# Attention with memory and a long convolution in one kernel: wider transfers, weights on a second queue, one operation for four products, row halves, and a new order

## The chip, the cores and the metric

The kernel runs on one core of a Trainium2 chip. The metric is the time of one execution in microseconds of the device (us). The engines are TensorE (PE in the profile; PEld is its loading of weights), VectorE (DVE), ScalarE (ACT), GpSimd (POOL) and SyncE (SP), whose queue (SPq) issues transfers. Each engine works through its own list in order and waits there for what the others deliver.

## The reference

Two independent parts whose outputs stand side by side, 2048 rows of 576 columns each, in bf16.

```python
def _A_ref(x, wq, wk, wv, wo, beta):       # S = 2048, D = 576, H = 32, Dh = 18, N = 4 segments of L = 512
    q, k, v = (x @ wq), (x @ wk), (x @ wv)           # split in heads and segments
    phi = lambda t: jnp.where(t > 0, t + 1.0, jnp.exp(t))
    g = _sigmoid(beta)
    for s in range(N):
        p = _softmax(qs @ ks.T * scale + mask)       # causal inside a segment
        a_dot = p @ vs
        a_mem = (phi(qs) @ M) / (phi(qs) @ z + 1e-06)
        o = g * a_mem + (1.0 - g) * a_dot
        M = M + phi(ks).T @ vs;  z = z + phi(ks).sum()
    return concat(o) @ wo
def _B_ref(q, k, v, shift_k, ssm_k, ssm_D):
    k_shift = short_conv(k, shift_k)                 # 4 taps
    kv = k_shift * v
    y = irfft(rfft(kv) * rfft(ssm_k)) + kv * ssm_D   # along the 2048 rows, per channel
    return q * y
```

## The kernel before

Part A goes through four segments of 512 rows. Per segment, x comes in transposed (tiles xT, line 737, one transposing load for each of five channel blocks); TensorE forms q and k for five blocks of up to 126 channels (seven heads of 18) and v for four row blocks. The contraction over 576 channels is five products of 128: the last block starts at channel 448, and the weights' overlapping rows are zeroed (line 607). q and k are copied from PSUM into tiles dn, written to a DRAM scratch (qk_scratch, line 768) and read back as pad tiles (line 778), in which each head has 32 partitions, so that four heads share TensorE's rows. Per group of four heads (hg, eight in a segment) there are three score steps (products at line 966, ScalarE's exponential at line 973 into P tiles, GpSimd's causal mask at line 980), the product with V, whose column of ones gives the sums of the softmax, a copy into a tile ou and a write to a_scratch (line 1026). The sums are read from a_scratch (cs, line 1040), inverted (lines 1046 and 1047) and spread by a product (R). The outputs come back in am tiles (line 1068), are scaled (line 1074), the memory part is added (line 1083), and the projection with wo follows. The memory part needs phi of q and k (lines 798, 804, 810), one operation for each of both.

Part B convolves k with its four taps as products with diagonal matrices (dg, line 404), multiplies by v (line 422), and writes kv to a DRAM scratch. The long convolution is a factored Fourier transform by products, in five channel groups. In each octave the transforms H (of the kernel) and X (of kv) are copied from PSUM and multiplied: lines 525, 529 and 530 give the four products of real and imaginary halves in tiles PQ. The inverse follows (Z), one transposing transfer per group (CT, line 558), a last product, and the multiplication by q (line 585).

The order of all steps is a table in the file: TURN says which step comes when, ENGINE which engine does it, SLOT which buffer it gets. Tiles rotate in a fixed number of slots (SLOTS), for example three pad tiles and five xT tiles. All transfers are issued on SP's queue in the order of the table. Nothing is planned at run time; an engine waits if what it needs is late.

## Time and profile before

| | |
|---|---|
| median of 3 runs | 341.86 us (341.12 to 344.55) |
| span of the profiled execution | 344.8 us |
| TensorE busy | 270.6 us (78%), granted clock 0.931 in the mean |
| VectorE busy | 244.9 us (71%) |
| ScalarE busy | 247.3 us (72%) |
| GpSimd busy | 105.8 us (31%) |
| transfers on the queues of SP | 71.7% of 16 engines' span, 51.99 MB |

A share of the span is an average over a start that fills the tables, a long middle in which both parts run mixed, and an end in which only the last segment and group are left. The chain that ended last follows, from the last instruction back, what each step was waiting for; its shares tell what the span was spent on. A time in a row is the start, counted from the span's begin, if it stands first.

### The profile page before, as it was taken

To read this page: it belongs to the slowest core of one execution; us is meant where nothing else is said; L and a number is where in the kernel's file an instruction comes from. 1 tells how busy PE (TensorE), PEld (TensorE's weight loads), DVE (VectorE), ACT (ScalarE), POOL (GpSimd) and SP (SyncE) were. 2 spreads that over 40 slices of the span, in tenths; PEclk is the share of its full clock that TensorE was granted. 3 is DMA by queue.
4 is the path that set the end of the run, shared out by engine and by line. 5 is a ranking of instruction groups with operands and counts; after the bars stand their busy time and mean duration, and the time that the engine had idled before them with its cause. 6 is when DMAs were issued, how large, how long until landed. Compare 5 with 4: busy or idle time off the path is not lost.

```text
span 344.8 us, 9276 instructions
## 1 busy us (share of the span) xinstructions
PE 270.6 (78%) x3850; PEld 167.3 (49%) x3855; DVE 244.9 (71%) x400; ACT 247.3 (72%) x290; POOL 105.8 (31%) x150
## 2 busy tenths in 40 slices
PE   1759789788978468989988978989877878868256
PEld 0335366345636325645645664545456646627123
DVE  4675677679999518877988884868768868866250
ACT  0484998587889425958979896998896849969302
POOL 9370022333332211222214235443601414413200
PEclk9998999899999969999999998999999969967858
DMA  5987889759969968892599855963694656573623
GB/s 138 279 115 155 191 130 155 196 110 163 193 182 195 188 153 212 155 205 60 164 192 130 248 92 163 197 171 92 135 165 132 130 165 120 95 177 80 139 57 84
DMA packets 132184, 52.58 MB, mean 152 GB/s; under 512 B 112430, under 2 KB 124910, under 8 KB 132142
## 3 DMA queue, kind: packets, MB, share of 16 engines
q1 hardware_dynamic: 132142, 51.99, 71.7%
q8 instruction: 30, 0.49, 0.7%
q14 instruction: 12, 0.10, 0.1%
HBM read 22.39 MB, written 17.01 MB: 114 GB/s over the span
## 4 chain that ended last, share of the span: by engine, by line
PE 30%; DMA 20%; ACT 18%; DVE 15%; SPq 12%; issue 5%; POOL 0%; DVEq 0%; ACTq 0%
PE PS L136 18%; ACT P L973 14%; PE PS L138 8%; DMA am<-a_scratch 5%; SPq L737 5%; DMA pad<-qk_scratch 5%; PE PS L966 3%; DMA CT<-Z 3%; DMA a_scratch<-ou 2%; DMA X<-in_B_v_dram 2%; DMA skb<-in_B_shift_k_dram 2%; DVE am L1074 2%; DVE dn L144 1%; ACT A L142 1%; DVE xs L315 1%
## 5 line engine op out<-in xcount | busy, mean ns | idle before, releaser
L973 ACT ACTIVATE P<-PS 128x1024 bf16<-128x1024 f32 x160 | 154.2, 1035 | 43.6 <-PE PS L966 33.4
L980 POOL TENSOR_SCALAR_AFFINE_SELECT P<-P 128x512 bf16<-128x512 bf16 (+1 forms) x112 | 79.5, 725 | 199.1 <-ACT P L973 116.8
L966 PE MATMUL PS<-pad 18*128 18x128 bf16 (+3 forms) x512 | 35.9, 314 | 12.5 <-DMA pad<-qk_scratch 5.7
L136 PE MATMUL PS<-xT,wq 128*126 128x512 bf16 (+1 forms) x100 | 28.4, 415 | 11.6 <-DMA xT<-in_A_x_dram 11.1
L966 PEld LDWEIGHTS <-pad 18*128 18x128 bf16 x512 | 11.2, 93 | 36.2 <-issue 26.8
L136 PE MATMUL PS<-wo,am 126*128 126x288 bf16 (+1 forms) x160 | 26.7, 322 | 2.4 <-DVE am L1083 1.1
L136 PE MATMUL PS<-X,dg 128*128 128x512 bf16 x75 | 21.6, 416 | 7.6 <-DMA X<-in_B_k_dram 6.3
L138 PE MATMUL PS<-P,V 128*32 128x256 bf16 (+3 forms) x512 | 23.8, 307 | 4.4 <-ACT P L973 1.6
L136 PE MATMUL PS<-xT,wk 128*126 128x512 bf16 (+1 forms) x100 | 26.6, 400 | 0.5 <-DMA wk<-in_A_wk_dram 0.4
L144 DVE CAST dn<-PS 126x1024 bf16<-126x1024 f32 (+1 forms) x16 | 19.5, 1219 | 9.4 <-ACT P L973 4.4
L138 PE MATMUL PS<-G,PQ 64*128 64x128 bf16 (+1 forms) x640 | 23.5, 225 | 3.3 <-ACT P L973 1.7
L138 PEld LDWEIGHTS <-Ft 128*64 128x64 bf16 x704 | 21.2, 114 | 7.2 <-issue 6.4
L138 PEld LDWEIGHTS <-PQ 64*128 64x128 bf16 (+1 forms) x640 | 20.5, 102 | 8.4 <-issue 7.0
L136 PE MATMUL PS<-wv,xT 128*128 128x288 bf16 x160 | 22.6, 291 | 2.2 <-ACT V L142 1.5
L138 PE MATMUL PS<-A,Ft 128*64 128x128 bf16 (+1 forms) x640 | 22.6, 223 | 2.0 <-ACT P L973 1.0
L138 PE MATMUL PS<-W,xs 128*64 128x128 bf16 x576 | 20.9, 220 | 4.1 <-ACT P L973 2.3
L136 PEld LDWEIGHTS <-wq 128*126 128x126 bf16 (+1 forms) x100 | 13.3, 141 | 21.2 <-issue 9.4
L144 DVE CAST A<-PS 128x1024 bf16<-128x1024 f32 x18 | 21.6, 1217 | 2.7 <-PE PS L138 2.6
L422 DVE TENSOR_TENSOR X<-PS,X 128x1024 bf16<-128x1024 f32 x10 | 12.1, 1222 | 15.7 <-PE PS L136 14.2
L138 PEld LDWEIGHTS <-xs 128*64 128x64 bf16 x576 | 17.9, 109 | 9.0 <-issue 7.8
L136 PEld LDWEIGHTS <-am 126*128 126x128 bf16 (+1 forms) x160 | 16.8, 109 | 11.2 <-issue 3.0
L804 ACT ACTIVATE fe<-dn 126x512 bf16<-126x512 bf16 (+1 forms) x30 | 19.1, 639 | 2.4 <-DVE fk L810 1.9
(127 smaller groups left out, 427.5 us busy)
## 6 DMA issues: line engine op xcount, KB each, us to landing
pad<-qk_scratch SPq DMA_DIRECT2D x32, 256.0 KB
a_scratch<-ou SPq DMA_DIRECT2D x32, 128.0 KB
qk_scratch<-dn SPq DMA_DIRECT2D x16, 252.0 KB
out_dram<-oA SPq DMA_DIRECT2D x16, 144.0 KB
xs<-in_B_ssm_k_dram SPq DMA_DIRECT2D x4, 512.0 KB
kv_scratch<-X SPq DMA_DIRECT2D x4, 512.0 KB
xs<-kv_scratch SPq DMA_DIRECT2D x4, 512.0 KB
q<-in_B_q_dram SPq DMA_DIRECT2D x8, 256.0 KB
```

Source lines behind the costliest of these rows:

```text
L136: self.nc.tensor.matmul(out, lhsT=lhsT, rhs=rhs, start=start, stop=stop)
L138: self.nc.tensor.matmul(out, lhsT=lhsT, rhs=rhs, start=start, stop=stop, tile_position=pos)
L142: self.nc.scalar.copy(out=out, in_=in_)
L144: self.nc.vector.tensor_copy(out=out, in_=in_)
L315: v.tensor_scalar(out=self.i32(ix), in0=self.i32(it), scalar1=self.t(self.bcol)[:, 0:1], scalar2=self.t(off)[:, 0:1], op0=ALU.mult, op1=AL ...
L422: self.nc.vector.tensor_tensor(out=self.t(kv)[:, sl], in0=self.psf(pc), in1=self.t(vT)[:, sl], op=ALU.mult)
L737: self.nc.sync.dma_start_transpose(out=self.t(b)[:], in_=self.A_x[0, L * s:L * s + L, c0:c0 + P])
L804: self.nc.scalar.activation(out=self.t(fe)[0:M], in_=self.t(dense[m])[0:M, w_, :], func=ACT.Exp)
L966: nc.tensor.matmul(o, lhsT=t[r, 1, q0:q0 + P], rhs=t[r, 0, q0:L], start=True, stop=True, tile_position=(32 * j, 0))
L973: self.nc.scalar.activation(out=out2(jj), in_=self.psf(pso[jj]), func=ACT.Exp, scale=scale)
L980: self.nc.gpsimd.affine_select(out=ap, in_=ap, compare_op=ALU.is_ge, fill=0.0, base=0, pattern=pat + [[1, P]], channel_multiplier=-1)
L1074: self.nc.vector.tensor_tensor(out=self.t(b)[0:M], in0=self.psf(pR)[0:M], in1=self.t(b)[0:M], op=ALU.mult)
```

## The change

- x of a segment comes in by two transposing loads, one of 512 channels and one of channels 448 to 575; a small copy inside SBUF puts the last 64 channels on the lower 64 partitions too. xT is one tile of one slot.
- The weights wq, wk, wv, wo, the short kernel, D and beta are loaded by ScalarE's queue (16 issues, 13 of them ahead of the first exponential); all else stays on SP's. The last 64 rows of wq are on the upper 64 partitions, those of wk on the lower, wv has half of its columns on each. The zeroing of line 607 is gone.
- q and k of a block: eight products of 128 rows and then one pair of products of 64 rows, q on the upper, k on the lower half of TensorE's rows, into different PSUM banks. v likewise, with its two column halves.
- A head's 18 channels lie as 9 and 9 in its 32 partitions (rows 0 to 8 and 16 to 24); a transfer's outer dimension is then 14 and not 7. Score products run over 25 rows, 7 of them zero. There are two scratches for q and k in turn, each filled with zeros once (four fills, not two). Pads come in pairs of head groups (16 loads of 512 KB for 32 of 256 KB), in two slots.
- ou holds a pair of head groups: 16 writes to a_scratch for 32. The softmax sums go from ou to cs by transfers inside SBUF, 16 for 9. Reciprocals are one operation a segment in the first three segments, two in the last (five for nine).
- The denominators of the memory part are written twice (six writes for three), since a head is in two halves.
- phi of q and k is one operation of 1024 where both are wanted (segments 1 and 2).
- The four spectral products are one operation of 2048 that reads each half of X and H twice.
- dg and the addition of the memory part may run on GpSimd; the fills of V with ones move from the program's first place into the order.
- SLOTS change (PQ two of 2048 and X two for PQ four of 1024; Hx 3 for 4, fe, rs, rb, rc one for two, am 5 for 6), and TURN, ENGINE and SLOT are new throughout.

Core of the diff:

```diff
-                    self.nc.sync.dma_start_transpose(out=self.t(b)[:], in_=self.A_x[0, L * s:L * s + L, c0:c0 + P])
+                self.nc.sync.dma_start_transpose(out=self.t(xT)[:, 0:4, :], in_=self.A_x[0, L * s:L * s + L, 0:512])
+                self.nc.sync.dma_start_transpose(out=self.t(xT)[:, 4, :], in_=self.A_x[0, L * s:L * s + L, 448:576])
+                self.nc.sync.dma_start(out=self.t(xT)[0:64, 4, :], in_=self.t(xT)[64:128, 4, :])
...
-                        for t in range(5):
-                            self.mm(o[0:M, w_, :], self.t(wt)[:, t, 126 * m:126 * m + M], self.t(xT[t])[:], t == 0, t == 4)
+                        for t in range(4):
+                            self.mm(o[0:M, w_, :], self.t(wt)[:, t, 126 * m:126 * m + M], x[:, t, :], t == 0, False)
+                        if w_ == 1:
+                            for i in range(2):
+                                w = self.t(self.w[("wq", "wk")[i]])
+                                r = slice(64 - 64 * i, 128 - 64 * i)
+                                self.mm(o[0:M, i, :], w[r, 4, 126 * m:126 * m + M], x[r, 4, :], False, True, (64 - 64 * i, 0))
...
-                    src = bass.AP(d.tensor, d.offset + hg * 128 * 1024, [[1024, P], [1, 1024]])
+                    src = bass.AP(d.tensor, d.offset + hp * 256 * 1024, [[1024, P], [128 * 1024, 2], [1, 1024]])
...
-                    self.nc.vector.tensor_tensor(out=self.t(Pt)[:], in0=self.t(X)[:], in1=self.t(H)[:], op=ALU.mult)
-                    self.nc.vector.tensor_tensor(out=x[:, 0:512], in0=x[:, 0:512], in1=h[:, 512:1024], op=ALU.mult)
-                    self.nc.vector.tensor_tensor(out=x[:, 512:1024], in0=x[:, 512:1024], in1=h[:, 0:512], op=ALU.mult)
+                        d = [[512, 2], [0, 2]]
+                        return bass.AP(a.tensor, a.offset, [list(a.ap[0]), d[i], d[1 - i], [1, 512]])
+                    self.nc.vector.tensor_tensor(out=self.t(Pt)[:].rearrange("p (a b f) -> p a b f", a=2, b=2), in0=dup(self.t(X), 0),
+                                                 in1=dup(self.t(H), 1), op=ALU.mult)
...
-                    src = bass.AP(d.tensor, d.offset + (4 * ha * 32 + DH) * L, [[32 * L, 4 * (hb - ha)], [P, 4], [1, P]])
-                    self.nc.sync.dma_start(out=self.t(cs)[16 * ha:16 * hb, :], in_=src)
+                        a = self.rows(self.t(ou), 25, 0, [(1, 32, 4), (0, P, 8), (0, 1, P)])
+                        self.nc.sync.dma_start(out=self.t(cs)[16 * (hg - 1):16 * (hg - 1) + 32, :], in_=a)
...
-    nV=6, splits=[[(0, 4), (4, 8)], [(0, 4), (4, 8)], [(0, 4), (4, 8)], [(0, 4), (4, 6), (6, 8)]]
+    nV=6, splits=[[(0, 8)], [(0, 8)], [(0, 8)], [(0, 4), (4, 8)]]
```

The lists of the engines, at three places. First SP's queue at the start of the program. Before, five loads of xT, two of wq and one of wk stand ahead of these rows (wk, wv: weights; X: transposed k and v of part B; P: the zeros; dn: q and k; skb, Dt: small constants):

```order
L615 DMA wk<-in_A_wk_dram 64x576
L612 DMA wv<-in_A_wv_dram 128x4x576
L615 DMA wv<-in_A_wv_dram 64x576
L721 DMA qk_scratch<-P_4_141 32x4x1792 x2
L375 DMA skb<-in_B_shift_k_dram 128x4
L370 DMA skb<-in_B_shift_k_dram 128x4x4
L389 DMA_TRANSPOSE X_1_100<-in_B_k_dram 128x2048
L768 DMA qk_scratch<-dn_119 7x18x1024
L364 DMA Dt<-in_B_ssm_D_dram 4x144x1
L768 DMA qk_scratch<-dn_120 7x18x1024
L392 DMA_TRANSPOSE X_0_99<-in_B_v_dram 128x2048
L778 DMA pad_130<-qk_scratch 128x1024
```

Now these are its first rows:

```order
L763 DMA_TRANSPOSE xT_113<-in_A_x_dram 128x4x512
L766 DMA_TRANSPOSE xT_113<-in_A_x_dram 128x512
L769 DMA xT_113<-xT_113 64x512
L398 DMA_TRANSPOSE X_0_99<-in_B_k_dram 128x2048
L750 DMA qk_scratch_160<-P_0_129 32x4x1792
L401 DMA_TRANSPOSE X_1_100<-in_B_v_dram 128x2048
L807 DMA qk_scratch_160<-dn_115 14x9x1024
L807 DMA qk_scratch_160<-dn_114 14x9x1024
L464 DMA xs_103<-in_B_ssm_k_dram 128x32x64
L817 DMA pad_121<-qk_scratch_160 128x2x1024
```

The weights and small constants are gone from it, the transposed load of v stands ahead of the first write of q and k, and the first pad is the tenth transfer instead of the twenty-first.

Second, SP's queue near the end. Before, the last two writes of ou were followed by the transpose of Z and then by the sums cs and the last two am:

```order
L1068 DMA am_142<-a_scratch 126x1x512
L1026 DMA a_scratch<-ou_157 128x512
L1026 DMA a_scratch<-ou_158 128x512
L558 DMA_TRANSPOSE CT_98<-Z_101 128x32x64
L1040 DMA cs_167<-a_scratch 32x1x128
L1068 DMA am_143<-a_scratch 72x1x512
L1068 DMA am_145<-a_scratch 126x1x512
```

Now (am_136 to am_138 are the last three of five):

```order
L1076 DMA a_scratch<-ou_148 128x2x512
L601 DMA out_dram<-q_102 64x16x128
L1076 DMA a_scratch<-ou_147 128x2x512
L1083 DMA cs_155<-ou_147 32x1x128
L601 DMA out_dram<-q_102 64x16x128
L1118 DMA am_136<-a_scratch 126x1x512
L1154 DMA out_dram<-oA_150 128x576
L1118 DMA am_137<-a_scratch 72x1x512
L1118 DMA am_138<-a_scratch 126x1x512
L576 DMA q_102<-in_B_q_dram 64x16x64
L567 DMA_TRANSPOSE CT_98<-Z_101 128x32x64
```

The sums follow the last write at once, and the transpose of Z stands behind the am loads.

Third, VectorE in the first octaves of the spectral products (PS is PSUM, Hx the kernel's transform, PQ the products). Before:

```order
L144 CAST PQ_112<-PS 128x1024
L798 TENSOR_SCALAR fq_125<-dn_119 126x512
L525 TENSOR_TENSOR PQ_111<-PQ_112,Hx_106 128x1024
L144 CAST PQ_109<-PS 128x1024
L529 TENSOR_TENSOR PQ_112<-PQ_112,Hx_106 128x512
L530 TENSOR_TENSOR PQ_112<-PQ_112,Hx_106 128x512
```

Now:

```order
L539 TENSOR_TENSOR PQ_110<-X_109,Hx_106 128x2048
L411 MEMSET X_1_100 128x8
L413 TENSOR_SCALAR dg_112<-ident,skf 128x128 x4
L145 CAST dn_114<-PS 126x1024
L145 CAST Hx_107<-PS 128x1024
L539 TENSOR_TENSOR PQ_111<-X_109,Hx_106 128x2048
```

Three operations have become one, and X has tiles of its own.

## Rows read from the trace of the kernel before

**Rows 1.** Busy times by stretch; columns: stretch, length, engines, clock, DMA share, GB/s.
```profile
0.00:36.00 36.00, 22.08 (x107) 12.43 (x108) 21.96 (x53) 16.14 (x20) 16.91 (x27) 0.95 0.80 174
36.00:320.00 284.00, 236.97 (x3666) 147.92 (x3672) 216.09 (x338) 226.85 (x264) 87.94 (x122) 0.95 0.75 155
```

**Rows 2.** The page's part 4: shares of the chain that ended last.
```profile
PE 30%; DMA 20%; ACT 18%; DVE 15%; SPq 12%; issue 5%; POOL 0%; DVEq 0%; ACTq 0%
PE PS L136 18%; ACT P L973 14%; PE PS L138 8%; DMA am<-a_scratch 5%; SPq L737 5%; DMA pad<-qk_scratch 5%; PE PS L966 3%; DMA CT<-Z 3%; DMA a_scratch<-ou 2%; DMA X<-in_B_v_dram 2%; DMA skb<-in_B_shift_k_dram 2%; DVE am L1074 2%; DVE dn L144 1%; ACT A L142 1%; DVE xs L315 1%
```

**Rows 3.** Timeline of the start; columns: start us, us, engine, line, operation.
```profile
23.13 4.09 SPq L392 DMA_TRANSPOSE X<-in_B_v_dram  x1
...
27.35 0.49 SPq L778 DMA_DIRECT2D pad<-qk_scratch  x1
...
36.23 1.94 ACT L973 ACTIVATE P<-PS 128x1024 bf16<-128x1024 f32 x2 [0.48 <-PE PS L966]
```

**Rows 4.** Instructions on one tile (PQ); columns: minimum/median/maximum ns.
```profile
L525 DVE TENSOR_TENSOR PQ<-PQ,Hx x18: 675/685/1146, 69.8 to 311.1; 128x1024 bf16<-128x1024 bf16 x18
L529 DVE TENSOR_TENSOR PQ<-PQ,Hx x18: 404/417/1258, 73.0 to 311.8; 128x512 bf16<-128x512 bf16 x18
```

**Rows 5.** Groups by line; columns: count, busy us, mean ns, idle before.
```profile
L144 DVE CAST A<-PS 128x1024 bf16<-128x1024 f32 x18 | 21.6, 1217 | 2.7 <-PE PS L138 2.6
...
L804 ACT ACTIVATE fe<-dn 126x512 bf16<-126x512 bf16 (+1 forms) x30 | 19.1, 639 | 2.4 <-DVE fk L810 1.9 <-DVE dn L144 0.4
...
L1046 DVE RECIPROCAL rc<-cs 64x128 f32<-64x128 bf16 (+1 forms) x9 | 8.5, 943 | 8.2 <-DMA cs<-a_scratch 8.2
...
L1083 DVE TENSOR_TENSOR am<-am,nm 126x512 bf16<-126x512 bf16 (+1 forms) x10 | 5.4, 547 | 0.1
```

**Rows 6.** Timeline of TensorE's products around 55 us.
```profile
54.87 1.29 PE L136 MATMUL PS<-xT,wq 128*126 128x512 bf16 x5
56.09 0.39 PE L966 MATMUL PS<-pad 18*128 18x512 bf16 x4
56.42 1.29 PE L136 MATMUL PS<-xT,wk 128*126 128x512 bf16 x5
```

**Rows 7.** The chain that ended last, in order of time; columns: start, us, what.
```profile
106.85 5.76 DMA pad<-qk_scratch
...
122.30 1.13 SPq L737
...
204.96 2.74 DMA xT<-in_A_x_dram
...
251.11 3.78 PE PS L136 x30
...
255.86 3.38 DMA a_scratch<-ou
...
259.31 1.96 DMA cs<-a_scratch
...
271.93 6.25 DMA pad<-qk_scratch
```

**Rows 8.** Two lines of transposing loads on SyncE's queue; minimum/median/maximum ns.
```profile
L737 SPq DMA_TRANSPOSE xT<-in_A_x_dram x20: 1127/1252/2441, 0.8 to 205.0; - x20
...
L392 SPq DMA_TRANSPOSE X<-in_B_v_dram x5: 1956/2678/4087, 23.1 to 148.3; - x5
```

**Rows 9.** Timeline of SyncE's queue near the end.
```profile
321.92 1.69 SPq L1026 DMA_DIRECT2D a_scratch<-ou  x2
323.65 3.08 SPq L558 DMA_TRANSPOSE CT<-Z  x1
326.85 1.24 SPq L1040 DMA_DIRECT2D cs<-a_scratch  x1
328.47 1.46 SPq L1068 DMA_DIRECT2D am<-a_scratch  x2
```

**Rows 10.** What SyncE's queue waited for; columns: us in total, times, longest.
```profile
SPq L778 <- PE PS L966: 6.6, 7, 1.5
```

More of the change, by code (lines that the diff above doesn't have):

```diff
@@ L160, in dma, with q, rows @@
         work = nb / pk * per[k] / eng
-        return self.g.add(name, {"SP": issue}, fn, r=r, w=w, prio=prio, lat=lat, work=work * self.p["dmaw"], al=al)
+        return self.g.add(name, {q: issue for q in queues}, fn, r=r, w=w, prio=prio, lat=lat, work=work * self.p["dmaw"], al=al)
+    def q(self, e):
+        return self.nc.sync if e == "SP" else self.nc.scalar
+    def rows(self, t, row, off, dims):
+        a = t[:]
+        n = a.ap[0][0]
+        return bass.AP(a.tensor, a.offset + row * n + off, [[k * n, c] if isr else [k, c] for isr, k, c in dims])
     def pe(self, name, cols, nmm, fn, r, w, prio, mode="F", al=()):
@@ L627, in build_a_consts, with vz @@
-                self.dma(nm + "4", l2, [], [(b, 1)], pr, 72 * 1152, pk=1152)
-        self.Vones = []
-        for i in range(p["nV"]):
-            pass
+                    self.q(e).dma_start(out=self.t(b)[0:72, 4, :], in_=self.A_wo[504:576, :])
+                self.dma(nm, l1, [], [(b, 0)], pr, 504 * 1152, pk=1152, queues=CQ)
+                self.dma(nm + "4", l2, [], [(b, 1)], pr, 72 * 1152, pk=1152, queues=CQ)
+        self.vz = F("vz")
+        def vz(e):
+            for i in range(SLOTS["V"]):
+                self.nc.gpsimd.memset(self.tiles[("V", i)][:], 1.0)
@@ L633, in build_a_consts, with lb0 @@
+        g.add("vz", {"POOL": 2.5}, vz, w=[self.vz], prio=p["prio_w"] - 30)
         self.gg = F("gg")
         bt = F("bt")
-        def lb(e):
-            src = bass.AP(self.A_beta.tensor, self.A_beta.offset, [[1, 32], [0, 4], [1, 1]])
-            self.nc.sync.dma_start(out=self.t(bt)[:], in_=src)
-        self.dma("beta", lb, [], [bt], p["prio_w"] + 20, 256, pk=64)
+        gd = Buf(None, "gd")
+        def lb0(e):
+            b, d = self.A_beta, self.tiles["gd"][:]
+            for u in range(2):
+                self.q(e).dma_start(out=bass.AP(d.tensor, d.offset + u, [[8, 4], [2, 4], [1, 1]]),
+                                    in_=bass.AP(b.tensor, b.offset + 4 * u, [[8, 4], [1, 4], [1, 1]]))
@@ L713, in build_a @@
             pieces[hg] = pcs
-        qd = Buf(None, "qd")
+        qd = [Buf(None, "qd%d" % i) for i in range(2)]
         zz = Buf("P4", "zz")
@@ new lines, in build_a, with f1 @@
+                ws = slice(1, 2) if s == 0 else slice(0, 1) if s == 3 else slice(0, 2)
+                n = L * (ws.stop - ws.start)
+                fm, fe = Buf("f", "f"), Buf("fe", "fe")
+                ff.append(fm)
+                def f1(e, fm=fm, m=m, M=M, ws=ws, dense=dense):
+                    self.nc.vector.tensor_scalar(out=self.t(fm)[0:M, ws, :], in0=self.t(dense[m])[0:M, ws, :], scalar1=0.0, scalar2=1.0,
+                                                 op0=ALU.max, op1=ALU.add)
@@ new lines, in build_a, with f2, f3 @@
+                g.add("phm%d.%d" % (s, m), {"DVE": c_ts4(n)}, f1, r=[dense[m]], w=[fm], prio=pr)
+                def f2(e, fe=fe, m=m, M=M, ws=ws, dense=dense):
+                    self.nc.scalar.activation(out=self.t(fe)[0:M, ws, :], in_=self.t(dense[m])[0:M, ws, :], func=ACT.Exp)
+                g.add("phe%d.%d" % (s, m), {"ACT": c_act(n)}, f2, r=[dense[m]], w=[fe], prio=pr)
+                def f3(e, fm=fm, fe=fe, M=M, ws=ws):
+                    v = self.t(fm)[0:M, ws, :]
+                    self.nc.vector.tensor_tensor(out=v, in0=v, in1=self.t(fe)[0:M, ws, :], op=ALU.min)
@@ L814, in build_a @@
+                g.add("pha%d.%d" % (s, m), {"DVE": c_tt2(n)}, f3, r=[fe], w=[fm], prio=pr)
             for tt in range(4):
@@ L969, in score @@
                     cols = sum(L - P * kt for kt, _, _ in which)
-                    g.add(nm, {"PE": cols / 2400.0 + 0.05 * len(which) + 0.03}, sc, r=list(pds.values()), w=pso, prio=pr, mode="R32", al=[self._pw])
+                    g.add(nm, {"PE": cols / 2400.0 + 0.05 * len(which) + 0.03}, sc, r=[pds], w=pso, prio=pr, mode="R32", al=[self._pw])
                     for jj in range(2):
@@ L1047, in rr_ @@
                     v.tensor_scalar(out=self.t(rb)[sl], in0=self.t(rc)[sl], scalar1=self.t(self.gg)[sl, 0:1], scalar2=None, op0=ALU.mult)
-                g.add("rs%d.%d" % (s, ha), {"DVE": 1.1}, rr_, r=[(cs, ha), self.gg], w=[rc, (rb, (ha, hb))], prio=pr)
+                g.add("rs%d.%d" % (s, ha), {"DVE": 1.1}, rr_, r=[(cs, k) for k in range(ha // 2, hb // 2)] + [self.gg], w=[rc, (rb, (ha, hb))], prio=pr)
             for m in range(5):
@@ L1233 @@
     pr.B_q, pr.B_k, pr.B_v, pr.B_sk, pr.B_h, pr.B_D, pr.out = B_q, B_k, B_v, B_shift_k, B_ssm_k, B_ssm_D, out
-    for i in range(SLOTS["V"]):
-        nc.gpsimd.memset(pr.tiles[("V", i)][:], 1.0)
     for o in order:
```

392 lines of the change are left out of this document (198 added, 194 removed).

## The prediction

> **What bounds the kernel now.** I read the busy times by stretch first. The span is 344.8 us; the sums below are made against it, since the rows are from that execution. The runs shown have a median of 341.86 us (341.12 to 344.55), 0.991 of the span, and a result in span time is multiplied by 0.991 at the end. Three stretches are to be seen: a start of 36 us until the first exponential, a middle of 284 us [rows 1], and the 24.8 us that are left for the end. In the middle TensorE is busy 237.0 us (83%), ScalarE 226.9 (80%), VectorE 216.1 (76%): no engine is full, and TensorE, the fullest, has 47 us of idle time. The chain that ended last [rows 2] shows what fills these holes: 48% of it is PE and ACT, but 20% lies in transfers and 12% in the queue of SyncE (SPq), which issues nearly every transfer in the order of the table. So 32% of the chain (110 us) is waiting for data and for its issue; this the change works on most. VectorE has 15% of the chain, so a us saved there is worth about 0.15 us, at 18% on ScalarE 0.18, on TensorE 0.30.
>
> **The start.** The first exponential runs at 36.23 [rows 3]. Its pad tile is issued at 27.35, right behind a transposing load of v that holds the queue from 23.13 for 4.09. The change takes the weights, the short kernels and beta from SP to ScalarE's queue, and turns five transposes of x into two. A transpose of 128x512 holds SP 1.252 us in the median, one of 128x2048, which has as many elements as the wide one of the change, 2.678, and 4.09 in the start [rows 8, 3]. SP's new queue to the pad is, from 0.8: wide x 4.1, last channels 1.25, a wait of about 2 for their landing (an estimate below the 2.74 us that the chain waits for a transpose of x, [rows 7]), copy 0.6, k 4.1, fill 0.65, v 4.1: 17.6. Then come two writes of q and k, which need the casts; ScalarE and VectorE reach these no sooner than now, because the sine tables stand ahead of them and ScalarE's own DMA issues (13 of the 16, at some 0.6 us each, with waits for earlier landings) stand between the sines. I take 18 to 20 for the writes, 2.5 for their landing, and the pad at about 22.5: 4.9 before 27.35. I take -5. Bounds: 0, since the same bytes must come in (174 GB/s over the start, [rows 1]) and the first pad is now twice as large; -9, if ScalarE has cleared its list by 27.
>
> **The middle, term by term.**
> Spectral products: one octave costs 685 + 2 x 417 = 1519 ns, and 512 more elements cost 685 - 417 = 268 ns [rows 4]. One operation of 2048 is then 685 + 2 x 268 = 1221 ns: 18 octaves save 18 x 0.30 = 5.4 us of VectorE. This holds if the repeated halves are read at the same rate. The other bound is one element a cycle, nearest row the PSUM cast of 1024 at 1217 ns [rows 5]: 2 x 1217 = 2434, which costs 18 x 0.92 = 16.5 us more. I take the first, since the inner run is 512 contiguous bf16 elements as in the 1024 row. The Trainium skill, VectorE: DVE Perf Modes, section What auto-detection actually checks, asks for 16-bit tensors with step 1, which points to the fast rate too; no run here shows a repeated operand yet.
> Feature maps: 20 of 30 operations pair up into 10. ScalarE saves 10 x (2 x 0.639 - 0.97) = 3.1 us ([rows 5]; 0.97 is half of the 1.94 of two exponentials in [rows 3]); VectorE about 10 x (2 x 0.417 - 0.685) = 1.5 for the minimum, and as much for the maximum: 3.
> Softmax reciprocals: 9 become 5, 4 x 0.943 = 3.8 us of VectorE [rows 5]. Additions of the memory part: 10 on VectorE become 3, 7 x 0.547 = 3.8 us, moved to GpSimd, which is busy 87.9 of the 284 us [rows 1]. Eight of 20 diagonal builds go there too, about 2. Against that, by the order, VectorE gets about 2 us more of evacuations and 1.3 of split masks. VectorE in all: -5.4 - 3 - 3.8 - 3.8 - 2 + 2 + 1.3 = -14.7. On the chain at 0.15: -2.2. (The 2, 2 and 1.3 are estimates: the counts in the two orders by the durations of like operations.) ScalarE: -3.1, about -2 for evacuations handed over, and two table loads less (2.6) that fall in the start; two issues of wo and two of beta add some 2 in the middle: -3, worth -0.5.
> Row halves on TensorE: 20 groups of ten 512-column products become nine rounds, 16 groups of ten 288-column products likewise. A product of 288 columns takes 0.126 (30 in 3.78, [rows 7]), one of 512 by that rate 0.224, so this would save 20 x 0.224 + 16 x 0.126 = 6.5 us. But each pair stands between products of the full array, and a change of form has a price: five full products from 54.87 to the next form at 56.09 take 1.22 where 5 x 0.224 is 1.12, so 0.10; from there to the next change at 56.42 one round of 512 columns, 0.224, takes 0.33, so 0.11 [rows 6]. At two changes for each of 36 pairs that is 72 x 0.11 = 7.9 us: +1.4 net, worth +0.4 on the chain. Bounds: -6.5 (no price) and +7.9 (the halves don't overlap). The Trainium skill, TensorEngine Tiling (Array Packing), section Key Properties, says that a change of tiling mode drains the engine; by that rule with this row's price the term is a loss, and by the columns alone it is the gain of 6.5.
> Transfers on the chain: the waits for pads are three, 5.76 and 6.25 the longer ones [rows 7], 15.6 together. Two scratches instead of one let the next segment's q and k be written while pads of this one are still to be read; half of these 15.6 goes, -6 to -8: I take -6.5. Transposes of x hold 5% of the chain [rows 2], 9.2 us of it in seven pieces at two later segment changes, the first at 122.30 [rows 7]; 5 x 1.25 = 6.3 becomes 2.68 + 1.25 = 3.9, which saves 0.38 of it: -3.5. Column sums go straight from the ou tile and no longer wait for a_scratch: 3.38 in front of 1.96 goes [rows 7]: -3.4. Attention outputs and pads in halves as many issues, the weights elsewhere: in SP's own slack, at nothing; what covers them is the rest of its queue, and uncovered they would be 32 issues of 0.49 us [rows 3].
> Sum of the middle: -2.2 - 0.5 + 0.4 - 6.5 - 3.5 - 3.4 = -15.7. Behind a removed wait stands an engine that is 80% full, so I keep about three quarters: **-12**. Bounds 0 and -27 (all of it, the other half of the pad waits, and TensorE's 6.5 at 0.30).
>
> **The end.** Now the last a_scratch writes are issued at 321.92, a transpose of Z follows at 323.65, column sums at 326.85, and the last two am loads at 328.47 [rows 9]. After the change the column sums are issued right behind the write and the am loads stand ahead of the transpose: am at 326.5, some 2 us sooner, but one of the last additions is on GpSimd, which is no faster than VectorE's 0.547, and may take some back. I take **-2** (0 to -4).
>
> **Sum.** 344.8 - 5 - 12 - 2 = 325.8 us of span, times 0.991: **323 us**.
>
> **The rivals.**
> A, more gain: the waits fall as a whole. -9 - 27 - 4 = -40 is the far end; its middle, -9 - 20 - 3 = -32, gives 310 us. For it: TensorE's 237 us leave room. Against: DMA queues are busy 75% of the middle [rows 1], and the CT and X transposes are not touched.
> B, the waits removed were not the last ones: another engine or transfer stands just behind each. Then half of the start is kept, -2.5, TensorE costs +1.4, the end gives nothing: -1.1, 341 us. For it: three engines at 76 to 83%.
> C, slower: pads. Two slots of two head groups replace three of one; a load can be issued only after the last score of a whole pair, and SP stands still until then, with am, a_scratch, rd and the next transposes behind it. Today such waits for scores are 6.6 us in 7 places, 1.5 the longest [rows 10]. There are 14 such loads; from 1.4 us each on the path (19 us) the gain is gone, and at 2 us each it is +28 - 19 = +9: 351 us. For it: whole-tile xT has the same fault. Against: the lookahead is still one pair, about 15 us of work.
> D, the slow rate of the products (+16.5 of VectorE instead of -5.2): 21.9 x 0.15 = 3.3 worse, 326 us; it is inside the forecast's own range.
>
> **How the numbers follow.** The forecast with D has a chance of 0.62 and its own range of 313 to 335; A 0.14; B 0.11; C 0.13. The predicted time is that of the forecast. The range of 303 to 343 takes in the forecast, B and most of A, and leaves out C and the far part of A, under 2 in 10. A change under 1% (338.4 to 345.3) can't be told from none here. Faster: 0.62 + 0.14 = 0.76; within 1%: B, 0.11; slower: C, 0.13.
>
> **What would show it.** The first exponential near 31; VectorE's middle near 201 us, the 2048-wide product near 1.23 us; TensorE's busy time in the middle within 5 us of 237.0; pad waits on the chain below 10 us; SP's L817 waiting for scores under 10 us in all; column sums issued right behind the last write. It is wrong if the first exponential stays at 36 (then -5 is lost), if the chain fills with pads (C), or if the transfers' share stays at 20%.

## The result, and the profile after

The changed kernel takes 312.76 us in the median of five runs (311.95 to 315.54), the kernel before 342.21 in runs beside it; the ratio is 0.9145, 95% interval 0.9097 to 0.9192. The forecast was 323 with a range of 303 to 343, so the time lies in the range, 10 us below the forecast and 3 us above rival A. The profiled execution spans 313.8 us where the one before spanned 344.8; it is the slowest of the five (315.54 us). Medians and ratios, here and below, leave out executions that ran over 1.5% above their kernel's fastest; that leaves run e9 two executions of four, and e8 no profiled one, so its stages are not given.

The sum came out near, but two of its parts did not. Here are both kernels by stretch: start to first exponential, first to last exponential, end. (Columns as in [rows 1]: stretch, length, busy us of TensorE, its weight loads, VectorE, ScalarE, GpSimd; granted clock, DMA share, GB/s.) First the kernel before:

```profile
0.00:36.23 36.23, 22.31 (x108) 12.55 (x110) 22.19 (x53) 16.14 (x21) 16.91 (x27) 0.95 0.80 174
36.23:319.63 283.40, 236.37 (x3659) 147.57 (x3663) 215.52 (x337) 226.48 (x264) 87.64 (x121) 0.95 0.74 155
319.63:344.80 25.17, 11.93 (x88) 7.17 (x87) 7.22 (x12) 4.67 (x8) 1.23 (x2) 0.73 0.39 91
```

And the changed one:

```profile
0.00:41.67 41.67, 24.59 (x151) 12.51 (x154) 21.11 (x48) 16.35 (x20) 18.56 (x34) 0.88 0.83 163
41.67:288.36 246.69, 225.82 (x3443) 135.47 (x3447) 193.37 (x260) 219.23 (x247) 99.28 (x134) 0.97 0.78 178
288.36:313.80 25.44, 16.41 (x265) 11.40 (x258) 13.95 (x18) 7.65 (x10) 5.91 (x5) 0.90 0.59 126
```

The start is 5.4 us longer, not 5 shorter; the middle is 36.7 shorter, not 12; the end is the same (+0.3), not 2 shorter. Together -31.0 us of span. In the middle TensorE is now busy 225.8 of 246.7 us, 92% where it was 83%. Over the whole span VectorE's busy time fell by 16.5 us (14.7 forecast) and ScalarE's by 4.1 (3 forecast for the middle). TensorE's fell by 3.8 where 1.4 more was forecast. Busy time multiplied by the mean granted clock, an estimate of its work at full speed, is 270.6 x 0.931 = 251.9 before and 266.8 x 0.948 = 252.9 now: by this estimate the 3.8 us are the higher clock and not less work.

On TensorE the 36.7 us of the middle are 10.6 of busy time (4.5 of it is now in the end, 2.3 in the start, 3.8 is the fall just named) and 26.1 of idle time. By what ended each wait, that idle time is 14.7 us less waiting for transfers, 8.1 less for VectorE (11.3 to 3.2) and 2.6 less for ScalarE (16.3 to 13.7). These are TensorE's waits for transfers between the first and the last exponential, before (engine and line waited, for what: us in total, times, longest):

```profile
PE PS L136 <- DMA X<-in_B_k_dram: 6.3, 1, 6.3
PE PS L966 <- DMA pad<-qk_scratch: 5.7, 4, 2.6
PE PS L138 <- DMA CT<-Z: 2.7, 1, 2.7
PE PS L136 <- DMA xT<-in_A_x_dram: 1.8, 1, 1.8
```

and after, the only one:

```profile
PE PS L1013 <- DMA pad<-qk_scratch: 1.8, 1, 1.8
```

16.5 us have become 1.8. The waits for CT and for X, which no edit of an operation touches, are gone too. The longest wait on the chain before was the transpose of Z in group 3 (start, us, what):

```profile
298.05 8.68 DMA CT<-Z
306.77 1.92 PE PS L138 x7
```

In the old table this transpose stands three steps ahead of the product that reads it, in the new one 35; for group 2 it is two steps and 38. But the table does not put every transfer farther ahead: in groups 0 and 1 it was 59 and 50 steps and is 61 and 33, and in group 4 two and one, where TensorE waited 7.4 us in the end before and does not wait now. What it takes away is most of the short leads; a pad's shortest is 1 step before and 10 now, its median 27 and 29. The k of group 3, for which TensorE waited 6.3 us, stood 31 steps ahead and stands 42. From its issue to its product 4.4 us passed before, and 10.3 pass now:

```profile
118.89 2.21 SPq L389 DMA_TRANSPOSE X<-in_B_k_dram  x1
...
123.25 0.59 PE L136 MATMUL PS<-X,dg 128*128 128x512 bf16 x1 [6.28 <-DMA X<-in_B_k_dram]
```

```profile
80.24 3.65 SPq L398 DMA_TRANSPOSE X<-in_B_k_dram  x1
...
90.49 1.02 PE L137 MATMUL PS<-X,dg 128*128 128x512 bf16 x3
```

So a lead in steps does not tell the lead in time; SyncE's queue itself can be late. After the change no product waits for a CT (one line's instructions; then what its engine waited for):

```profile
L139 PE MATMUL PS<-CT,Psi x36: 376/403/635, 137.3 to 305.9; 128*64 128x512 bf16 x36
...
  ACT P L1020: 0.3, 1
```

Why the start is longer stands in SyncE's and ScalarE's lists. SyncE (start us, us):

```profile
2.24 3.03 SPq L766 DMA_TRANSPOSE xT<-in_A_x_dram  x1
10.95 0.56 SPq L769 DMA_DIRECT2D xT<-xT  x1
...
16.53 3.52 SPq L401 DMA_TRANSPOSE X<-in_B_v_dram  x1
26.47 1.84 SPq L807 DMA_DIRECT2D qk_scratch<-dn  x2
...
31.62 1.14 SPq L817 DMA_DIRECT2D pad<-qk_scratch  x1
```

The copy of the last channels waits 5.7 us for x to land; the writes of q and k come at 26.47, not at 18 to 20, and the first pad at 31.62, not at 22.5 (27.35 in [rows 3]). They wait for casts, and these for weights that ScalarE issues late (the value in brackets is the idle time before, and what ended it):

```profile
12.98 0.53 ACTq L623 DMA_DIRECT2D wq<-in_A_wq_dram  x1
...
20.04 0.68 PE L139 MATMUL PS<-xT,wq 64*126 64x512 bf16 x1 [6.40 <-DMA wq<-in_A_wq_dram]
...
20.20 0.52 ACTq L623 DMA_DIRECT2D wv<-in_A_wv_dram  x1
...
21.40 1.06 ACT L331 ACTIVATE Ft<-xs 128x1024 bf16<-128x1024 int32 x1 [9.96 <-issue]
```

The last rows of wq are issued at 12.98 and waited for until 20.04, 7 us. ScalarE itself does nothing from 11.44 to 21.40, because its next issue (wv) does not come before 20.20 and the sine stands behind it in the list. What holds that issue back until then, the view does not show.

### The profile page after: what moved, and what is told of

Same layout as the page of the kernel before. It is cut to its first block, busy times and chain, and to the rows that moved or that the text cites. A ratio compares the mean times of both kernels' runs of the same rounds, so it can differ in the third digit from the quotient of the medians.

```text
span 313.8 us, 9204 instructions
## 1 busy us (share of the span) xinstructions
PE 266.8 (85%) x3848; PEld 159.4 (51%) x3855; DVE 228.4 (73%) x324; ACT 243.2 (78%) x276; POOL 123.8 (39%) x171
## 5 line engine op out<-in xcount | busy, mean ns | idle before, releaser
L1027 POOL TENSOR_SCALAR_AFFINE_SELECT P<-P 128x512 bf16<-128x512 bf16 (+1 forms) x112 | 84.1, 771 | 145.5 <-ACT P L1020 120.5
L1013 PE MATMUL PS<-pad 25*128 25x512 bf16 (+3 forms) x512 | 37.8, 307 | 5.3 <-DMA pad<-qk_scratch 1.8
L137 PE MATMUL PS<-xT,wq 128*126 128x512 bf16 (+1 forms) x80 | 22.9, 416 | 9.9 <-DMA xT<-in_A_x_dram 8.7
L539 DVE TENSOR_TENSOR PQ<-X,Hx 128x2048 bf16<-128x2048 bf16 x18 | 26.2, 1453 | 0.6 <-ACT Hx L143 0.6
L1013 PEld LDWEIGHTS <-pad 25*128 25x128 bf16 x512 | 11.6, 92 | 26.9 <-issue 21.0
L145 DVE CAST dn<-PS 126x1024 bf16<-126x1024 f32 (+1 forms) x13 | 15.9, 1223 | 12.2 <-PE PS L139 7.2
L137 PE MATMUL PS<-xT,wk 128*126 128x512 bf16 (+1 forms) x80 | 23.6, 422 | 0.0
L143 ACT CAST A<-PS 128x1024 bf16<-128x1024 f32 x18 | 18.3, 1024 | 2.7 <-PE PS L139 2.7
L137 PE MATMUL PS<-X,dg 128*128 128x512 bf16 x73 | 19.1, 381 | 0.9 <-ACT P L1020 0.5
L1133 POOL TENSOR_TENSOR am<-am,nm 126x512 bf16<-126x512 bf16 (+1 forms) x12 | 15.8, 1331 | 9.0 <-DVE am L1124 9.0
```

What stands on the lines that cost most here:

```text
L137: self.nc.tensor.matmul(out, lhsT=lhsT, rhs=rhs, start=start, stop=stop)
L143: self.nc.scalar.copy(out=out, in_=in_)
L145: self.nc.vector.tensor_copy(out=out, in_=in_)
L539: self.nc.vector.tensor_tensor(out=self.t(Pt)[:].rearrange("p (a b f) -> p a b f", a=2, b=2), in0=dup(self.t(X), 0), in1=dup(self.t(H), 1) ...
L1013: nc.tensor.matmul(o, lhsT=t[r, 1, q0:q0 + P], rhs=t[r, 0, q0:L], start=True, stop=True, tile_position=(32 * j, 0))
L1027: self.nc.gpsimd.affine_select(out=ap, in_=ap, compare_op=ALU.is_ge, fill=0.0, base=0, pattern=pat + [[1, P]], channel_multiplier=-1)
```

## Experiments

The theory after the result, **T**: the new table issues transfers in better time for their readers, and the middle got shorter by that. Its rival, **R**: the operations themselves (wider transfers, one operation for several) carried the gain. All runs keep the table unless said. The stages of every run, cut like those above, with the ratio to the kernel before:

| run | median us | ratio (95%) | start | middle | end |
|---|---|---|---|---|---|
| before | 342.21 | 1 | 36.23 | 283.40 | 25.17 |
| changed | 312.76 | 0.9145 (0.9097 to 0.9192) | 41.67 | 246.69 | 25.44 |
| e1, all operations undone | 339.48 | 0.9875 (0.9820 to 0.9930) | 35.93 | 268.99 | 33.08 |
| e5, all but the sums undone | 317.52 | 0.9235 (0.9153 to 0.9316) | 35.62 | 252.08 | 28.20 |
| e6, sums by a_scratch | 331.82 | 0.9695 (0.9635 to 0.9756) | 41.71 | 256.17 | 31.02 |
| e9, the same, read later | 319.11 | 0.9295 (0.9194 to 0.9396) | 42.17 | 248.70 | 26.83 |
| e10, before, sums by SBUF | 349.52 | 1.0147 (1.0038 to 1.0256) | 36.22 | 285.12 | 26.06 |
| e4, three weights on SP | 307.45 | 0.8949 (0.8880 to 0.9018) | 35.00 | 247.03 | 26.47 |
| e7, narrow transfers | 319.65 | 0.9325 (0.9260 to 0.9390) | 40.18 | 251.44 | 27.18 |
| e12, narrow x alone | 318.75 | 0.9278 (0.9187 to 0.9368) | 40.73 | 251.04 | 26.73 |
| e11, one scratch | 310.08 | 0.9028 (0.8948 to 0.9107) | 41.83 | 242.12 | 24.95 |
| e2, three products | 316.63 | 0.9191 (0.9121 to 0.9261) | 43.03 | 245.69 | 27.38 |
| e3, full rows | 310.61 | 0.9044 (0.8989 to 0.9099) | 41.73 | 239.74 | 27.93 |
| e8, e3 and e4 together | 306.08 | 0.8915 (0.8848 to 0.8982) | | | |

The kernel before was run beside each group of four (342.4 to 344.5 in the median), so differences are taken between ratios; 0.01 is 3.4 us. The stages are those of one execution each.

**Operations undone, table kept (e1, e5).** The edits of e1 are those shown singly below, with 32 pad loads, 32 writes of ou, phi in two operations and all weights on SP. Here and in e6 beta keeps its former order while the rows of the sums have another, so that heads are weighed by another head's gate; the work is the same.

> The new order of work kept, the operations of before put back: three spectral products per octave, last 64 channels on the full array with zeroed weights (four small fills more), x in five transposes, one scratch for q and k, 32 pad loads, 32 writes of ou, softmax sums read from a_scratch, phi one operation for each of q and k, weights and constants on SyncE's queue. Theory T (the middle got shorter because the new order issues each transfer well ahead of its reader): the sum of these parts is small, VectorE +5 (products) +3 (phi), ScalarE +3, worth 3 to 6 us with SyncE's longer list, and the start may win some back: 312 to 321 us. Rival R (the operations carried the gain): most of the 29 us comes back, 328 to 342 us.

339.48 us: nearly all comes back, as R had it. But one view of SyncE's waits held a cause that lay in how I had put the sums back (engine, line, for what: us, times, longest):

```profile
SPq L1089 <- DMA a_scratch<-ou: 33.1, 15, 4.2
```

Each read of the sums stood right behind the write that it needs, and SyncE's whole queue stood with it. e5 leaves this one part as changed:

> The first undo once more, with the softmax sums left as in the changed kernel (from ou, inside SBUF). In the first undo they were read from a_scratch right behind each write, and SyncE's queue stood 33.1 us in 15 places for these writes to land; this run tells that apart from the other parts. Theory T (the new order carries the middle's gain, the standing queue made the first undo slow): SyncE's waits for a_scratch are gone, and the time is 314 to 321 us. Rival R (the other operations carry it: narrow transfers, three products, one phi at a time): 330 us or more.

317.52 us, ratio 0.9235: as T had it. In its middle TensorE waits 4.4 us for transfers, where the kernel before waits 16.5; the two longer waits are

```profile
PE PS L1017 <- DMA pad<-qk_scratch: 2.4, 1, 2.4
PE PS L137 <- DMA X<-in_B_k_dram: 1.6, 1, 1.6
```

With narrow x, pads and writes, one scratch, three products, separate phi, full rows and the weights on SP, the new table still runs 26 us below the kernel before. Of these parts some cost and some gain (below), so 0.009 is their sum, not a proof that each is nothing. e1 and e5 differ in the sums alone: 0.064, 22 us.

**The sums (e6, e9, e10).**

> The changed kernel with only the softmax sums read from a_scratch instead of from ou, each read issued behind the write of its pair (the rows of the sums lie in another order, which the spreading matrix follows). Theory Q (a read that must wait for a write to land stops all that stands behind it on SyncE's queue): SyncE waits about 33 us more in 15 places, as in the first undo, and the time rises by 8 to 20 us, 321 to 333. Rival (SyncE has the slack, these waits cost only where the sums are needed): as my term of 3.4 for one such wait on the chain, 0 to 5 us more, 313 to 318.

```diff
-    a = self.rows(self.t(ou), 25, 0, [(1, 32, 4), (0, P, 8), (0, 1, P)])
+    d = self.tiles["ad"][s, hg - 1]
+    a = bass.AP(d.tensor, d.offset + 25 * L, [[32 * L, 8], [P, 4], [1, P]])
...
+        if at("cs%d" % i) < at("ad%d" % i):
+            put(["cs%d" % i], "ad%d" % i)
```

331.82, and SyncE waits as expected, at the expense of the middle and the end (9.5 and 5.6 us longer):

```profile
SPq L1084 <- DMA a_scratch<-ou: 40.6, 14, 4.6
```

Is it the standing queue or the late sums? e9 issues each read three transfers later:

> As the run with only the sums read from a_scratch (331.8 us), but each read issued three transfers later on SyncE's queue (fewer where the reciprocal comes first), so that the write has had time to land. Theory Q (the price is the standing queue): SyncE's wait for a_scratch falls from 40.6 us in 14 places to under 12 and the time to 314 to 320 us. Rival L (the price is that the sums come late, by DRAM's write and read): it stays at 326 us or more, since a later issue brings the sums later still.

```diff
+    for i in range(1, 32, 2):
+        put(["cs%d" % i], "ad%d" % i)
+        k, n = at("cs%d" % i), 0
+        rs = "rs%d.%d" % (i // 8, 4 if i >= 28 else 0)
+        while n < 3 and o[k + 1].name != rs:
+            o[k], o[k + 1] = o[k + 1], o[k]
+            n += o[k].eng == "SP"
+            k += 1
...
```

The first line of the loop sets the read behind its write, the rest moves it past three more transfers of SyncE, but not past the reciprocal; beta has the matching order here.

```profile
SPq L1084 <- DMA a_scratch<-ou: 1.6, 2, 0.8
```

The wait is gone and 0.040 of the 0.055 with it (319.11 us): theory Q, near the upper end of what it expected. Some 14 of the 19 us were the queue that stood; the rest, 5 us, is barely told from nothing (intervals 0.9194 to 0.9396 and 0.9097 to 0.9192). The Trainium skill, DMA: Bandwidth & Descriptors, section Anatomy of one DMA — SWDGE (gpsimd) path, says that the DMA engines wait on no semaphore and that such a wait happens in the issuing sequencer, ahead of the transfer. The section treats GpSimd's path; the 40.6 us on SyncE's queue agree. Then the part alone in the old order:

> The kernel before, with one part of the change alone: the softmax sums go from ou to cs inside SBUF, one small transfer right behind each of the 32 writes of ou, in place of 9 reads of a_scratch. SyncE waited 10.4 us in 4 places for these reads, and 3.4 + 2.0 us of them lay on the chain; 32 issues of 0.6 us (19) come for 9 of 1.2. If the part is worth in the old order what the undo says it is worth in the new one (0.055 of the time): 322 to 330 us. If it is worth its own waits there, as the prediction had it: 334 to 341 us, 0.975 to 0.997 of the kernel before.

```diff
     self.nc.sync.dma_start(out=self.tiles["ad"][s, hg], in_=self.t(ou)[:])
+    t = self.t(ou)[:]
+    n = t.ap[0][0]
+    src = bass.AP(t.tensor, t.offset + DH * n, [[32 * n, 4], [P, 4], [1, P]])
+    self.nc.sync.dma_start(out=self.t(cs)[16 * hg:16 * hg + 16, :], in_=src)
...
+                    return
```

The return leaves out the read of a_scratch.

349.52, ratio 1.0147 (1.0038 to 1.0256): above both expectations, and by the interval a little slower than before. There the reads waited 10.4 us in four places; that the 32 small issues cost more than that is likely, but was not measured alone. So the part is worth 19 us against reads that stand right behind their writes, some 5 against reads three transfers later, and nothing or less in the old order: what it gains depends on the table.

**The start (e4).**

> The changed kernel with three of the weight loads (the last 64 rows of wq, half of those of wv, and wv's main part) moved from ScalarE's list to SyncE's, right behind the two transposes of x. In the changed kernel wq's last rows are issued at 12.98 and TensorE waits for them until 20.04, ScalarE stands until 21.40, and the first exponential is at 41.67. Theory S (the late weights and ScalarE's standing at its issues cost the start): they land by about 11, the first exponential comes 4 to 7 us sooner, and the time falls by 3 to 6 us: 307 to 310. Rival B (the start is bound by the bytes of the transposes, whichever queue): the first exponential stays within 2 us of 41.7 and the time within 1.5 us of 312.8.

```diff
+    put(["wq40", "wv40", "wv"], "x4_0", "SP")   # behind x's second transpose, on SyncE's queue
```

307.45, ratio 0.8949, 0.020 (6.7 us) below the changed kernel. The first exponential comes at 35.00 and not at 41.67; the middle is the same (247.03). SyncE and ScalarE now:

```profile
5.47 0.60 SPq L623 DMA_DIRECT2D wq<-in_A_wq_dram  x1
...
15.15 1.06 ACT L331 ACTIVATE Ft<-xs 128x1024 bf16<-128x1024 int32 x1 [1.61 <-DVE xs L326]
...
16.48 0.68 PE L139 MATMUL PS<-xT,wq 64*126 64x512 bf16 x1
...
27.20 1.09 SPq L817 DMA_DIRECT2D pad<-qk_scratch  x1
```

wq's last rows are issued at 5.47 in SyncE's idle time, no product waits for them, the second sine comes at 15.15 and not at 21.40, the pad at 27.20. Theory S stands. e5, with all weights on SP, has its first exponential at 35.62 too. An issue that waits on ScalarE's queue holds ScalarE's sines up (the 9.96 us above), and the DMA engines are 0.83 busy in the start already. e4 changes the queue and the place of the three loads together; the same loads earlier on ScalarE's own list were not run.

**Narrow transfers (e7, e12, e11).**

> The changed kernel with its transfers narrow again: x in five transposes, 32 pad loads, 32 writes of ou, one scratch for q and k with two fills; the sums stay inside SBUF, weights on ScalarE's queue. SyncE gets 16 + 16 issues of about 0.5 us and 12 transposes of about 1.25 more, 31 us of issue in 314. Theory T (this lies in SyncE's slack, and the new order puts one scratch's writes behind the reads anyway): 1 to 4 us, 314 to 317. Rival R (as the prediction had it: pads 6.5, transposes 3.5 on the chain): 8 to 12 us more, 321 to 325.

319.65, 0.018 (6.2 us) slower: between both theories. e12 and e11 take it apart.

> The changed kernel with x in five transposes of 128 channels per segment instead of one of 512 and one of 128; 12 transposes more on SyncE's queue, at 1.25 us each, less the wide ones' 2.0. All narrow transfers together cost 0.018 of the time of the kernel before, 6.2 us. If the transposes are most of it (my term was 3.5): 316 to 319 us, 0.922 to 0.932 of the kernel before. If pads and writes in halves are: 312.5 to 314.5.

```diff
-    self.nc.sync.dma_start_transpose(out=self.t(xT)[:, 0:4, :], in_=self.A_x[0, L * s:L * s + L, 0:512])
+    for t in range(4):
+        self.nc.sync.dma_start_transpose(out=self.t(xT)[:, t, :], in_=self.A_x[0, L * s:L * s + L, P * t:P * t + P])
```

318.75, 0.0133 (4.5 us) slower, with intervals that just overlap (0.9187 to 0.9368 and 0.9097 to 0.9192): by these medians the transposes are most of it; my term was 3.5.

> The changed kernel with one scratch for q and k (two fills of zeros instead of four). The prediction gave two scratches 6.5 us, by pad waits on the chain. If that is their part, 317 to 320 us. If the new order puts every write of q and k behind the reads of the heads that it overwrites anyway, there is no new wait and SyncE saves two fills: 311 to 313.5.

```diff
+                    if i == 1:
+                        return
...
-    pr.tiles["qkd"] = [tc.dram_tile([H, 32, 1024], BF16, name="qk_scratch%d" % i) for i in range(2)]
+    pr.tiles["qkd"] = [tc.dram_tile([H, 32, 1024], BF16, name="qk_scratch")] * 2
```

The first two lines leave out the fills of the second scratch.

310.08, 0.0117 (4 us) faster than with two; the intervals (0.8948 to 0.9107 and 0.9097 to 0.9192) just touch. A second scratch brings nothing that shows here, and its fills may stand in the way. In the changed kernel two more of them are on SyncE's queue between the first pads:

```profile
55.28 0.79 SPq L750 DMA_DIRECT2D qk_scratch<-P  x1
...
69.39 0.56 SPq L750 DMA_DIRECT2D qk_scratch<-P  x1
...
78.54 1.65 SPq L817 DMA_DIRECT2D pad<-qk_scratch  x1
```

and with one scratch the same pad is issued 3 us sooner:

```profile
75.58 0.51 SPq L819 DMA_DIRECT2D pad<-qk_scratch  x1
```

If x costs 4.5 and one scratch gives 4 back, pads and writes in halves cost 5 to 6 in e7, which I had at nothing. This is a difference of three runs, each with an interval of 0.013 to 0.018 of the time, and was not measured alone.

**Products and row halves (e2, e3).**

> The changed kernel with only the spectral product of an octave in three operations (one of 1024 elements, two of 512) into the same tile. The median of the single one is 1.218 us, the three cost 0.685 + 2 x 0.417 = 1.52, so VectorE gets 18 x 0.30 = 5.4 us more. Theory T: VectorE is not what ends last in most of the middle, so at its share of the chain 1 us or less, 312.8 to 314.5. Rival R (the product is a link of the chain in every octave: TensorE's next products wait for it): 3 to 6 us more, 316 to 319.

```diff
-    self.nc.vector.tensor_tensor(out=self.t(Pt)[:].rearrange("p (a b f) -> p a b f", a=2, b=2), in0=dup(self.t(X), 0),
-                                 in1=dup(self.t(H), 1), op=ALU.mult)
...
+    v.tensor_tensor(out=own, in0=x[:].rearrange("p (a f) -> p a f", a=2), in1=h[:].rearrange("p (a f) -> p a f", a=2), op=ALU.mult)
+    v.tensor_tensor(out=q[:, 512:1024], in0=x[:, 0:512], in1=h[:, 512:1024], op=ALU.mult)
+    v.tensor_tensor(out=q[:, 1024:1536], in0=x[:, 512:1024], in1=h[:, 0:512], op=ALU.mult)
```

Ratio 0.9191 against 0.9145: 1.6 us more, and the intervals overlap (0.9121 to 0.9261 and 0.9097 to 0.9192). The expected 1 us or less isn't told from it; 3 to 6 us in the chain (R) isn't excluded by the time, but the middle does not grow (245.69).

> The changed kernel with the last 64 channels of q, k and v as products of the full array (weights zeroed on the rows not wanted, four small fills on GpSimd at the start), no row halves. Each of 36 pairs becomes two products one behind the other: 20 x 0.224 + 16 x 0.126 = 6.5 us more columns on TensorE. If a change of form costs 0.11 us as I took it, 72 changes or 7.9 us fall away and TensorE's busy time sinks by about 1.4; the time stays within 1 us of 312.8. If changes cost half of that or less, TensorE is 2.5 to 6.5 us busier and the time, with TensorE at 92% of the middle, rises by 2 to 5 us: 315 to 318.

```diff
-    r = slice(64 - 64 * i, 128 - 64 * i)
-    self.mm(o[0:M, i, :], w[r, 4, 126 * m:126 * m + M], x[r, 4, :], False, True, (64 - 64 * i, 0))
+    self.mm(o[0:M, i, :], w[:, 4, 126 * m:126 * m + M], x[:, 4, :], False, True)
...
+    for nm, r0, f0, f1 in (("wq", 0, 0, D), ("wk", 64, 0, D), ("wv", 0, 0, 288), ("wv", 64, 288, D)):
+        nc.gpsimd.memset(pr.tiles[nm][r0:r0 + 64, 4, f0:f1], 0.0)
```

310.61, 0.010 (3.5 us) faster; the intervals touch. I expected no change or a loss. The price of a form can be read behind the change (TensorE; start, us):

```profile
98.70 1.03 PE L137 MATMUL PS<-xT,wk 128*126 128x512 bf16 x4
99.66 0.43 PE L139 MATMUL PS<-xT,wq 64*126 64x512 bf16 x1
99.66 0.43 PE L139 MATMUL PS<-xT,wk 64*126 64x512 bf16 x1
99.92 1.06 PE L139 MATMUL PS<-G,PQ 64*128 64x128 bf16 x32
```

Four full products take 0.96 to the pair (4 x 0.224 is 0.90), the pair 0.26 to the next (one round is 0.224): 0.06 and 0.04 for the two changes, half of the 0.11 I took. By these rows the halves save 6.5 - 72 x 0.05 = 2.9 us of TensorE. Busy time scaled by the granted clock as above says a little less: 266.8 x 0.948 = 252.9 with halves, 262.8 x 0.966 = 253.9 without. So the halves do not cost TensorE work, and the 3.5 us lie elsewhere. One stretch of the profiled executions differs, 57 to 65 us, first changed, then e3, then e11:

```profile
57.00:65.00 8.00, 6.20 (x61) 2.84 (x60) 2.79 (x4) 3.80 (x5) 2.46 (x4) 0.79 1.15 266
```

```profile
57.00:65.00 8.00, 7.38 (x95) 4.16 (x97) 4.34 (x9) 6.73 (x9) 2.46 (x4) 1.00 1.13 246
```

```profile
57.00:65.00 8.00, 7.59 (x100) 3.73 (x98) 5.07 (x9) 6.93 (x9) 2.46 (x4) 1.00 1.22 218
```

In the changed kernel TensorE stands 1.80 us for a pad there and then runs partly at 1.2 GHz (granted clock 0.79); in the other two its longest wait between 50 and 70 us is 0.3 us, and the clock is 1.00. Whether the halves make that pad late, or chance does, stays open; the execution of the changed kernel that is shown was its slowest.

**Both (e8).**

> Both single edits that helped, together: full-array products for the last 64 channels and three weight loads on SyncE's list. By ratio to the kernel before the first gave 0.010 (3.5 us), the second 0.020 (6.7 us). If they are separate, one in the middle and one in the start, they add: about 0.885 of the kernel before, 302 to 304 us. If the row halves cost only because TensorE was late from the start, less adds: 305 to 307.

306.08, ratio 0.8915: the best measured, 11% below the kernel before and 2.5% below the changed one. Against e4 alone (0.8949) the gain of e3 is within the intervals, so that it adds is not shown.

## Why the prediction was right, and where not

**The start, -5, was wrong in sign (+5.4).** Two steps of the queue's sum failed: "a wait of about 2 for their landing" (5.7 measured; e4 keeps most of it, its copy is issued at 10.84, so it is not what e4 gives back), and that VectorE and ScalarE reach the writes "no sooner than now", with the writes then put at 18 to 20. I had named ScalarE's issues with waits for earlier landings between the sines, and gave them no price; ScalarE stands 9.96 us in one piece and TensorE waits 6.40 for a weight. e4 shows the late loads of weights to be the cause: 6.7 us come back with three issues moved.

**The middle, -12, was too small by 25 us.** VectorE's -14.7 and ScalarE's -3 were about right as work. TensorE's row halves, +1.4, are between 1.0 and 2.9 us the other way by the two estimates under e3. Of the 36.7 us some 7 are work that moved into the start and the end, which no term had. The terms of the transfers:
- *x transposes, -3.5*: 4.5 by e12, with intervals that just overlap. Right as far as that goes.
- *Pads by two scratches, -6.5*: wrong. TensorE's waits for pads did fall (5.7 to 1.8 us; the 15.6 of the prediction are the transfers' times on the chain, in part of which TensorE works), but e11 has no second scratch and its middle is not longer (242.12). I had credited the resource with what the order does.
- *Column sums, -3.4*: near the 5 us against reads three transfers later (e9). Against reads right behind their writes it is 19 (e6), and in the old order nothing or less (e10): the size hangs on the order, which the term did not have.
- *Pads and writes in halves, "at nothing"*: by difference some 5 us, not measured alone.
- *Three quarters kept, CT and X "not touched"*: the step that failed most. The change rewrote the table, and the table moves every transfer, touched or not: CT, X and am held 10 points of the chain [rows 2], 34 us, and no computing engine waits for any of them now; on TensorE in the middle CT and X were 9.0 of the 16.5 us. The discount for what stands behind each wait failed too: TensorE's waits for VectorE and ScalarE fell by 10.7 us with those for transfers, where the chain's shares gave both engines together 2.7. Why they fell was not tested.

**The end, -2**: nothing (+0.3). The sums are issued right behind the last write as forecast, and the last am loads 4.6 us behind it (295.32), as in the prediction. But TensorE has 4.5 us more work left in the end, and three of the last additions are on GpSimd, not one: two take it 3.17 us and a third 1.86, where VectorE needs 0.41 for one (its median for the same line). Which of the two took the 2 us back was not tested.

```profile
290.69 0.36 SPq L1076 DMA_DIRECT2D a_scratch<-ou  x1
291.10 0.79 SPq L1083 DMA_DIRECT2D cs<-ou  x1
```

```profile
293.66 3.17 POOL L1133 TENSOR_TENSOR am<-am,nm 126x512 bf16<-126x512 bf16 x2 [4.41 <-DVE am L1124]
```

**So the total was right by two errors that partly cancel**: +10.4 in the start against -24.7 in the middle. The middle went as rival A had it ("the waits fall as a whole"), which I gave 0.14, and beyond A's far end of -27; A's point against itself, that CT and X are not touched, was false.

**The rivals that fell.** B: no waits of like length stood behind those removed; TensorE's idle time in the middle fell by 26.1 us. C: SyncE waits 1.9 + 1.8 us for the scores of a pair, far from 1.4 for each of 14 loads:

```profile
SPq L817 <- PE PS L139: 1.9, 3, 1.2
...
SPq L817 <- PE PS L1013: 1.8, 2, 1.3
```

D: the repeated operand is read at the fast rate, median 1.218 us where 1.221 was forecast (the "-5.2" in D's sum is the -5.4 of the term). In all, 18 octaves took 31.0 us and take 26.2:

```profile
L539 DVE TENSOR_TENSOR PQ<-X,Hx x18: 1206/1218/3857, 66.9 to 293.5; 128x2048 bf16<-128x2048 bf16 x18
```

**The announced signs.** Right were the product near 1.23, the pad waits under 10 us (read on TensorE: the chain of the changed kernel is followed back to 262.85 us only, so its shares, and the sign of 20% in transfers, can't be read), L817's waits for scores under 10 (3.7), and the sums right behind the last write. Wrong was the first exponential near 31 (41.67). VectorE's middle, 201 announced, is 193.4 and TensorE's 225.8, not within 5 of 237, since more of the work now lies outside the middle (TensorE: 4.5 us in the end, 2.3 in the start).

**What is open.** The 26 us of e5 belong to the table together with the parts that e5 keeps: the sums by SBUF, heads in two halves, five reciprocals, additions and dg on GpSimd, other slots. The table names the operations of the changed kernel, so it can't be run with the old ones, and its share alone was not measured. The table also orders the engines' own work. No run moves the transfers alone in the old kernel, so that T's cause, the time of issue, carries the table's share is argued from TensorE's waits (16.5 us before, 4.4 in e5, 1.8 after) and not shown by itself.

## What to carry to other kernels

Where a change comes with a new order of all work, do not add up waits of the edited operations: list every wait of the chain, ask of each whether the new order issues it earlier against its reader, in time and not only in steps, and count those in. Price a transfer that must wait for another's landing by what stands behind it on its queue, not by its own wait: the same 16 reads cost 19 us right behind their writes and some 5 three places later. Loads that are given to a computing engine's queue belong on a queue that is idle then (e4); ahead of that engine's first work would be another way, which was not run.
